# Attention with top-k and a highway layer: two heads stacked on the partitions of kT and qT, score matmuls alternating between the two 64-row halves of the array

## Chip, cores and metric

One core of a Trainium2 chip runs the whole program. The metric is device microseconds of one execution. The kernel before takes 1702.07 us (median of 2 runs, 1701.22 to 1702.92). All single times below are in us.

## The reference, cut to what matters

```python
B, H, S, D = 8, 8, 576, 64                      # q, k, v in fp32
scores = scale * q @ k^T                        # per batch and head: 576 x 576
kth    = 32nd largest of each row
mask   = scores >= kth
attn   = softmax(where(mask, scores, -1e9))     # only 32 entries per row survive
x      = attn @ v        -> rows of B*S, 512 columns (all heads side by side)
out    = T * relu(x @ w_h) + (1 - T) * x,   T = sigmoid(x @ w_t + b_t)
```

The 32nd largest value decides exactly which scores survive, so scores stay in fp32.

## The kernel before

A query tile is 128 rows of one head (the last tile of a batch holds 64 rows of two heads). There are 288 such tiles, worked on in groups of three. Where 40 query tiles are counted below, one is the same rows for all eight heads (five in each of eight batches). For each tile VectorE (DVE) finds the 32nd largest value with four `max` (8 values each) and three `match_replace`, then multiplies the exponentials by the mask:

```python
def prep_head(prep, stages, h):                    # k and q of one head -> kT, qT
    for src_t, dst_t in ((kin, kT), (qin, qT)):
        for g0 in range(0, nck, 4):                # 512 columns, then 64
            kqps = fps.tile([P, max(dm, 512)], FP32, tag="fp")    # ONE buffer
            for c in range(g0, g1):
                nc.tensor.transpose(kqps[0:D, ...], src_t[0:kc, c, :], ident_f[...])
            nc.scalar.copy(dst_t[0:D, h, col0:col1], kqps[0:D, 0 : col1 - col0])

def attn_scores(b, qt, heads, kT, qT, tix):
    ps = bigps.tile([P, nck * P], FP32, tag="big")                # two buffers
    # ... for every head, s0 in (0, 512):
        nc.tensor.matmul(ps[...], qT[0:D, h, qs : qs + qlen], kT[0:D, h, s0:s1])
    nc.scalar.copy(sc, ps)                                        # scores to SBUF
    nc.scalar.activation(e, ps, AF.Exp, scale=scale)

# chain_emitter, on DVE: max, match_replace, max, match_replace, max, match_replace, max
nc.vector.scalar_tensor_tensor(out=ep, in0=sc, scalar=m4[:, 7:8], in1=e,
                               op0=ALU.is_ge, op1=ALU.mult)       # "the mask", line 218
nc.gpsimd.memset(ep[0:nrows, S : nck * P], 0.0)

# ... transposes of ep, product with v, and for a finished 128-row tile of all heads:
nc.vector.reciprocal(...); nc.vector.tensor_scalar_mul(rinv, rinv, 0.5)
nc.gpsimd.tensor_tensor(x, xs, rinv.to_broadcast(...), ALU.mult)
# FFN: 4 transposes (xtps), 4 matmuls (hps), 5 matmuls (tps), all in the "fp" buffer; then
nc.gpsimd.tensor_add(s1, h2, x)                   # four GpSimd ops with two SBUF inputs
nc.gpsimd.tensor_sub(h2, h2, x)
nc.gpsimd.tensor_mul(h2, h2, tt)
nc.gpsimd.tensor_add(o, s1, h2)
nc.gpsimd.dma_start(out_rows, o)
```

The loads of k, q and v of the next batch stand at the end of the first query tile of a batch (the later ones wait until staging memory comes free), and `prep_head` of the next batch is spread over its second and third query tiles, between the other work. The program fixes the order of TensorE's instructions.

The softmax here doesn't subtract the row's maximum and nothing guards it: scores larger than these inputs give would overflow.

## Time and profile before

| | before |
|---|---|
| time | 1702.07 |
| span in the profile | 1701.3 |
| DVE busy | 1633.3 (96%) |
| TensorE busy | 1304.4 (77%) |
| start-up idle of DVE (first five waits for scores) | 44.4 |
| the 288 masks on DVE | 241.8 |

The busy line of the page of the kernel before:

```profile
PE 1304.4 (77%) x5448; PEld 671.2 (39%) x5480; DVE 1633.3 (96%) x3248; ACT 730.9 (43%) x1529; POOL 436.1 (26%) x732
```

The view of waits of DVE in the kernel before (what waited, on whom: us in total, times, longest):

```profile
DVE m_396 L197 <- ACT sc L188: 29.7, 1, 29.7
DVE m_398 L197 <- ACT sc L188: 5.0, 1, 5.0
DVE m_400 L197 <- ACT sc L188: 5.0, 1, 5.0
DVE m_565 L197 <- ACT sc L188: 3.9, 1, 3.9
DVE rinv_all L266 <- ACT xs L259: 3.9, 1, 3.9
DVE m_981 L197 <- ACT sc L188: 0.8, 1, 0.8
```

These are all waits of DVE in the whole run. Five lie at the start (44.4 us together) and one at the end. From 113 us, where the wait of 0.8 us ends, to the last group DVE never waits. So a change pays only if it shortens the start, the tail, or the DVE instructions themselves.

The groups of the page that the change touches (line, engine, op, names, shapes, count; then busy us, mean ns; then idle before them and who ended it):

```profile
L181 PE MATMUL ps<-kT,qT 64*128 64x512 f32 (+3 forms) x1280 | 720.1, 723 | 8.3 <-ACT e L190 7.3
...
L160 PE MATMUL kqps<-ident_f,kin 128*64 128x128 f32 (+1 forms) x320 | 79.7, 366 | 59.3 <-ACT kT L165 29.1
L160 PE MATMUL kqps<-ident_f,qin 128*64 128x128 f32 (+1 forms) x320 | 81.8, 375 | 56.3 <-ACT qT L165 31.2
```

The score matmuls are the largest item of TensorE. The two groups of transposes are busy for 161 us, but TensorE stands idle for another 115 us just before them, mostly for the copy out of the single PSUM buffer (97 of the 115 us in the full view of these lines).

The view of one source line, the mask, over the whole run (window, DVE busy and count, then clock, DMA share, GB/s):

```profile
0.00:1702.00 1702.00, 241.79 (x288) 0.59 0.11 22
```

And the timeline around one finished query tile of the kernel before (start, length, engine, line, op; "idle before" in brackets; lines between left out):

```profile
619.06 0.18 DVE L266 RECIPROCAL rinv_all<-xs 128x8 f32<-128x8 f32 x1
...
627.95 1.26 POOL L318 TENSOR_TENSOR s_5360<-h_5356,x 128x512 f32<-128x512 f32 x1
629.29 1.27 POOL L319 TENSOR_TENSOR h_5356<-h_5356,x 128x512 f32<-128x512 f32 x1
...
633.10 1.26 POOL L320 TENSOR_TENSOR h_5356<-h_5356,tt 128x512 f32<-128x512 f32 x1 [2.54 <-ACT xs L259]
...
633.67 1.30 DVE L218 SCALAR_TENSOR_TENSOR ep<-sc,m_5430,e 128x576 bf16<-128x576 f32 x1
...
634.44 1.66 POOL L322 TENSOR_TENSOR o<-s_5360,h_5356 128x512 f32<-128x512 f32 x1
...
634.90 1.82 DVE L218 SCALAR_TENSOR_TENSOR ep<-sc,m_5432,e 128x576 bf16<-128x576 f32 x1
...
636.64 0.80 DVE L218 SCALAR_TENSOR_TENSOR ep<-sc,m_5434,e 128x576 bf16<-128x576 f32 x1
```

The third mask, with no FFN op beside it, takes 0.80 us. The first two overlap the last two FFN ops on GpSimd (POOL) and take 1.30 and 1.82 us. DVE counts this as busy time, so no wait shows it. The rule is in the Trainium skill, "SBUF — State Buffer", section "Who interferes with whom": a DVE instruction with two SBUF inputs contends with a GpSimd instruction that reads SBUF. This trace agrees: the mask has two such inputs (sc and e).

Two things decide when the FFN's ops run on GpSimd. The first is when x starts. In the program, the pad writes of the mask tiles (line 227) stand before x on GpSimd, and by the page they wait for TensorE's transposes of finished masks (line 238). In one tile whose reciprocal starts at 278.76 us, TensorE first prepares k and q of the next batch (until 282.84), and x starts 5.4 us after the reciprocal instead of 1.0 (page, then timelines):

```profile
L227 POOL MEMSET ep<- 128x64 bf16 x288 | 43.2, 155 | 1106.5 <-PE etall L238 1067.4
...
282.77 1.25 PE L238 MATMUL etall<-ident_b,ep 128*128 128x128 bf16 x10
...
284.08 0.15 POOL L227 MEMSET ep<- 128x64 bf16 x1 [0.38 <-PE etall L238]
284.19 1.03 POOL L269 TENSOR_TENSOR x<-xs,rinv_all 64x512 f32<-64x512 f32 x1
```

The second is how long TensorE takes for the FFN's products once x is there.

### The profile page before, as it was taken

To read this page: it belongs to the slowest core of one execution; us is meant where nothing else is said; L and a number is where in the kernel's file an instruction comes from. 1 tells how busy PE (TensorE), PEld (TensorE's weight loads), DVE (VectorE), ACT (ScalarE), POOL (GpSimd) and SP (SyncE) were. 2 spreads that over 40 slices of the span, in tenths; PEclk is the share of its full clock that TensorE was granted. 3 is DMA by queue.
4 is the path that set the end of the run, shared out by engine and by line. 5 is a ranking of instruction groups with operands and counts; after the bars stand their busy time and mean duration, and the time that the engine had idled before them with its cause. 6 is when DMAs were issued, how large, how long until landed. Compare 5 with 4: busy or idle time off the path is not lost.

```text
span 1701.3 us, 18714 instructions
## 1 busy us (share of the span) xinstructions
PE 1304.4 (77%) x5448; PEld 671.2 (39%) x5480; DVE 1633.3 (96%) x3248; ACT 730.9 (43%) x1529; POOL 436.1 (26%) x732
## 2 busy tenths in 40 slices
PE   3888877888678876889768886788877888686653
PEld 1444433443334433444334443344433443343322
DVE  0899999999999999999999999999999999999994
ACT  2445444553335543455335543455443544343432
POOL 7001125012340133321141111511115112131133
PEclk9997656555555565555555555555555555555555
DMA  7110002100110002110021000210002000000000
GB/s 132 39 32 28 7 8 27 31 28 7 15 27 23 28 11 16 34 31 14 7 18 42 28 7 7 28 31 28 7 7 28 25 7 7 7 10 1 7 13 10
DMA packets 71829, 36.60 MB, mean 22 GB/s; under 512 B 51888, under 2 KB 68272, under 8 KB 71728
## 3 DMA queue, kind: packets, MB, share of 16 engines
q0 software_dynamic: 41856, 14.17, 6.0%
q1 hardware_dynamic: 15008, 10.76, 2.2%
q10 hardware_dynamic: 14864, 10.49, 2.2%
q8 instruction: 44, 0.72, 0.2%
q14 instruction: 57, 0.47, 0.1%
HBM read 30.67 MB, written 9.44 MB: 24 GB/s over the span
## 4 chain that ended last, share of the span: by engine, by line
DVE 55%; PE 24%; issue 9%; POOL 5%; ACT 4%; ACTq 1%; DMA 1%; DVEq 0%; POOLq 0%
PE ps L181 11%; DVE ep L218 7%; PE kqps L160 5%; PE etall L238 2%; PE etall L251 2%; PE hps L290 1%; ACT qT L165 1%; POOL vbraw L128 1%; ACT kT L165 1%; PE tps L299 1%; POOL vbraw L139 1%; POOL vbraw L118 1%; PE xtps L280 1%; ACTq L128 1%; DMA wh_76<-in_moe_w_h_dram 0%
## 5 line engine op out<-in xcount | busy, mean ns | idle before, releaser
L181 PE MATMUL ps<-kT,qT 64*128 64x512 f32 (+3 forms) x1280 | 720.1, 723 | 8.3 <-ACT e L190 7.3
L238 PE MATMUL etall<-ident_b,ep 128*128 128x128 bf16 x1440 | 195.9, 304 | 221.2 <-DVE ep L218 218.5
L181 PEld LDWEIGHTS ps<-kT,qT 64*128 64x128 f32 (+1 forms) x1280 | 285.7, 283 | 198.3 <-issue 158.2
L227 POOL MEMSET ep<- 128x64 bf16 x288 | 43.2, 155 | 1106.5 <-PE etall L238 1067.4
L188 ACT COPY sc<-ps 128x576 f32<-128x576 f32 x288 | 186.3, 647 | 304.7 <-DVE ep L218 258.3
L238 PEld LDWEIGHTS <-ep 128*128 128x128 bf16 x1440 | 138.9, 137 | 275.0 <-DVE ep L218 239.3
L245 ACT COPY et<-etall 128x640 bf16<-128x640 bf16 x288 | 192.5, 697 | 74.5 <-PE etall L238 72.3
L190 ACT ACTIVATE e<-ps 128x576 bf16<-128x576 f32 x288 | 191.9, 666 | 0.0
L251 PEld LDWEIGHTS <-et 128*128 128x128 bf16 (+1 forms) x1600 | 101.2, 134 | 124.8 <-issue 36.4
L251 PE MATMUL etall<-vbraw,et 128*128 128x65 bf16 (+1 forms) x1600 | 124.3, 242 | 10.3 <-ACT et L245 9.9
L160 PE MATMUL kqps<-ident_f,kin 128*64 128x128 f32 (+1 forms) x320 | 79.7, 366 | 59.3 <-ACT kT L165 29.1
L160 PE MATMUL kqps<-ident_f,qin 128*64 128x128 f32 (+1 forms) x320 | 81.8, 375 | 56.3 <-ACT qT L165 31.2
L165 ACT COPY kT<-kqps 64x512 f32<-64x512 f32 (+1 forms) x128 | 50.3, 393 | 119.3 <-PE kqps L160 116.2
L259 ACT COPY xs<-etall 128x65 f32<-128x65 f32 (+1 forms) x288 | 59.8, 221 | 80.5 <-PE etall L251 77.1
L165 ACT COPY qT<-kqps 64x512 f32<-64x512 f32 (+1 forms) x128 | 50.2, 393 | 95.3 <-PE kqps L160 90.7
L160 PEld LDWEIGHTS kqps<-ident_f,kin 128*64 128x64 f32 (+1 forms) x320 | 39.7, 143 | 110.8 <-ACT kT L165 45.9
L160 PEld LDWEIGHTS kqps<-ident_f,qin 128*64 128x64 f32 (+1 forms) x320 | 41.4, 148 | 95.3 <-ACT qT L165 53.0
L316 ACT ACTIVATE tt<-tps 128x512 f32<-128x512 f32 (+1 forms) x40 | 23.8, 596 | 123.7 <-PE tps L306 123.7
L290 PE MATMUL hps<-wh,xT 128*128 128x512 bf16 (+1 forms) x128 | 67.2, 614 | 7.7 <-issue 6.8
L299 PE MATMUL tps<-wt,xT 128*128 128x512 bf16 (+1 forms) x160 | 65.2, 553 | 2.0 <-ACT h_14371 L314 0.7
L280 PEld LDWEIGHTS xtps<-ident_f,x 128*128 128x128 f32 (+1 forms) x160 | 27.7, 216 | 75.6 <-POOL x L269 70.0
L280 PE MATMUL xtps<-ident_f,x 128*128 128x128 f32 (+1 forms) x160 | 40.5, 407 | 20.2 <-POOL x L269 19.2
(3393 smaller groups left out, 2328.6 us busy)
## 6 DMA issues: line engine op xcount, KB each, us to landing
kin<-in_k_dram SPq DMA_DIRECT2D x64, 128.0 KB, 2.0
qin<-in_q_dram ACTq DMA_DIRECT2D x64, 128.0 KB, 2.1
out_dram<-o POOLq DMA_DIRECT2D x32, 256.0 KB, 2.6
vbraw<-in_v_dram POOLq DMA_DIRECT2D x64, 64.0 KB, 2.7
wt_79<-in_moe_w_t_dram ACTq DMA_DIRECT2D x1, 1024.0 KB, 9.4
wh_76<-in_moe_w_h_dram SPq DMA_DIRECT2D x1, 1024.0 KB, 8.3
kin<-in_k_dram ACTq DMA_DIRECT2D x64, 16.0 KB, 2.2
qin<-in_q_dram SPq DMA_DIRECT2D x64, 16.0 KB, 2.3
```

Source lines behind the costliest of these rows:

```text
L160: nc.tensor.transpose(kqps[0:D, (c - g0) * P : (c - g0) * P + kc], src_t[0:kc, c, :], ident_f[0:kc, 0:kc],)
L165: nc.scalar.copy(dst_t[0:D, h, col0:col1], kqps[0:D, 0 : col1 - col0])
L181: nc.tensor.matmul(ps[r0 : r0 + qlen, s0:s1], qT[0:D, h, qs : qs + qlen], kT[0:D, h, s0:s1],)
L188: nc.scalar.copy(sc[0:nrows, :], ps[0:nrows, 0:S])
L190: nc.scalar.activation(e[0:nrows, :], ps[0:nrows, 0:S], AF.Exp, scale=scale)
L218: nc.vector.scalar_tensor_tensor(out=ep[0:nrows, 0:S], in0=sc[0:nrows, :], scalar=m4[0:nrows, 7:8], in1=st["e"][0:nrows, :], op0=ALU.is_ge ...
L238: nc.tensor.transpose(etall[0:P, c * P : c * P + nrows], ep[0:nrows, c * P : (c + 1) * P], ident_b[0:nrows, 0:nrows],)
L245: nc.scalar.copy(et[0:P, 0:nck, 0:nrows], etps_v[0:P, 0:nck, 0:nrows])
L251: nc.tensor.matmul(pso[0:qlen, gi * DE : (gi + 1) * DE], et[0:P, c, q0 : q0 + qlen], vb[0:P, h, c, :], start=(c == 0), stop=(c == nck - 1),)
L280: nc.tensor.transpose(xtps[0:P, g * P : g * P + qlen], x[0:qlen, g * P : (g + 1) * P], ident_f[0:qlen, 0:qlen],)
L290: nc.tensor.matmul(hps[0:qlen, 0:dm], xT[0:P, g, 0:qlen], wh[0:P, g, 0:dm], start=(g == 0), stop=(g == n_g - 1),)
L299: nc.tensor.matmul(tps[0:qlen, 0:dm], xT[0:P, g, 0:qlen], wt[0:P, g, 0:dm], start=(g == 0), stop=False,)
```

## The change

The intent: a contraction of 64 rows fills half of the array. With an even head on rows 0 to 63 and its odd neighbour on rows 64 to 127, the score matmuls of the two heads can go to different halves and overlap. Staging two heads side by side also lets one transpose of 128 columns prepare both heads.

```diff
-        for h in range(H):
-            kin = ldpool.tile([P, nck, D], FP32)
-            qin = ldpool.tile([P, nck, D], FP32)
+        for hp in range(NHP):
+            kin = ldpool.tile([P, nck, 2, D], FP32)
+            qin = ldpool.tile([P, nck, 2, D], FP32)
+            for hh in range(2):
+                h = 2 * hp + hh
+                load_head(k, kin[:, :, hh, :], b, h, (nc.sync, nc.scalar))
+                # ... q and v alike
     def prep_alloc(b):
-        kT = kqpool.tile([D, H, S], FP32)
+        kT = kqpool.tile([P, NHP, S], FP32)
     # prep_head becomes prep_pair
                     nc.tensor.transpose(
-                        kqps[0:D, ...], src_t[0:kc, c, :], ident_f[0:kc, 0:kc])
-                nc.scalar.copy(dst_t[0:D, h, col0:col1], kqps[0:D, 0 : col1 - col0])
+                        kqps[:, ...], src_t[0:kc, c, :, :].rearrange("p h d -> p (h d)"), ...)
+                nc.scalar.copy(dst_t[:, hp, col0:col1], kqps[:, 0 : col1 - col0])
+    def score_pieces(qt, qlen, hp, outs, kT, qT):
+        for s0 in range(0, S, 512):
+            for hh in range(2):
+                r = slice(hh * D, (hh + 1) * D)
+                nc.tensor.matmul(outs[hh][:, s0:s1], qT[r, hp, qs : qs + qlen], kT[r, hp, s0:s1])
     # attn_scores: an even head takes both PSUM buffers and issues the pair's pieces,
     # the odd head finds its scores ready (cut)
     # schedule of the next batch's preparation: pairs instead of heads (cut)
```

The DVE instructions are the same in number and order.

More of the change, by code (lines that the diff above doesn't have):

```diff
@@ L133, in load_batch @@
         vb = vbraw[:, :, 0 : nck * DE].rearrange("p h (c e) -> p h c e", e=DE)
-        for h in range(H):
-            kin = ldpool.tile([P, nck, D], FP32)
-            qin = ldpool.tile([P, nck, D], FP32)
-            load_head(k, kin, b, h, (nc.sync, nc.scalar))
-            load_head(q, qin, b, h, (nc.scalar, nc.sync))
-            nc.gpsimd.memset(vbraw[:, h, :], 1.0)
-            load_head(v, vb[:, h, :, 0:D], b, h, (nc.gpsimd, nc.gpsimd))
+        for hp in range(NHP):
[4 more added lines that the diff above has]
+                load_head(k, kin[:, :, hh, :], b, h, (nc.sync, nc.scalar))
+                load_head(q, qin[:, :, hh, :], b, h, (nc.scalar, nc.sync))
+                nc.gpsimd.memset(vbraw[:, h, :], 1.0)
+                load_head(v, vb[:, h, :, 0:D], b, h, (nc.gpsimd, nc.gpsimd))
             stages.append((kin, qin))
@@ L144, in prep_alloc, with prep_pair @@
     def prep_alloc(b):
-        kT = kqpool.tile([D, H, S], FP32)
-        qT = kqpool.tile([D, H, S], FP32)
+        kT = kqpool.tile([P, NHP, S], FP32)
+        qT = kqpool.tile([P, NHP, S], FP32)
         return kT, qT
-    def prep_head(prep, stages, h):
+    def prep_pair(prep, stages, hp):
         kT, qT = prep
-        kin, qin = stages[h]
+        kin, qin = stages[hp]
         for src_t, dst_t in ((kin, kT), (qin, qT)):
@@ L160, in prep_head, with evac @@
                     nc.tensor.transpose(
-                        kqps[0:D, (c - g0) * P : (c - g0) * P + kc],
-                        src_t[0:kc, c, :],
+                        kqps[:, (c - g0) * P : (c - g0) * P + kc],
+                        src_t[0:kc, c, :, :].rearrange("p h d -> p (h d)"),
                         ident_f[0:kc, 0:kc],
                     )
-                nc.scalar.copy(dst_t[0:D, h, col0:col1], kqps[0:D, 0 : col1 - col0])
+                nc.scalar.copy(dst_t[:, hp, col0:col1], kqps[:, 0 : col1 - col0])
     def prep_batch(b, stages):
         prep = prep_alloc(b)
-        for h in range(H):
-            prep_head(prep, stages, h)
-        return prep
-    def attn_scores(b, qt, heads, kT, qT, tix):
-        qs = qt * P
-        qlen = chunk_len(qt)
-        ps = bigps.tile([P, nck * P], FP32, tag="big")
-        for gi, h in enumerate(heads):
-            r0 = gi * P2 if len(heads) > 1 else 0
-            for s0 in range(0, S, 512):
-                s1 = min(S, s0 + 512)
-                nc.tensor.matmul(
-                    ps[r0 : r0 + qlen, s0:s1],
-                    qT[0:D, h, qs : qs + qlen],
-                    kT[0:D, h, s0:s1],
-                )
-        nrows = P if len(heads) > 1 else qlen
+        for hp in range(NHP):
+            prep_pair(prep, stages, hp)
+        return prep
+    def evac(ps, nrows, tix):
         sc = scpool.tile([P, S], FP32, tag=f"sc{tix % NROT}")
@@ L190, in attn_scores @@
         nc.scalar.activation(e[0:nrows, :], ps[0:nrows, 0:S], AF.Exp, scale=scale)
-        return dict(sc=sc, e=e, nrows=nrows, qlen=qlen, heads=heads)
+        return sc, e
+    def score_pieces(qt, qlen, hp, outs, kT, qT):
+        qs = qt * P
+        for s0 in range(0, S, 512):
+            s1 = min(S, s0 + 512)
+            for hh in range(2):
+                r = slice(hh * D, (hh + 1) * D)
+                nc.tensor.matmul(
+                    outs[hh][:, s0:s1],
+                    qT[r, hp, qs : qs + qlen],
+                    kT[r, hp, s0:s1],
+                )
+    def attn_scores(b, qt, heads, kT, qT, tix):
+        qlen = chunk_len(qt)
+        hp = heads[0] // 2
+        if len(heads) > 1:
+            ps = bigps.tile([P, nck * P], FP32, tag="big")
+            score_pieces(qt, qlen, hp, [ps[0:P2, :], ps[P2:P, :]], kT, qT)
+            sc, e = evac(ps, P, tix)
+            return dict(sc=sc, e=e, nrows=P, qlen=qlen, heads=heads)
+        if heads[0] % 2 == 0:
+            pss = []
+            for hh in range(2):
+                ps = bigps.tile([P, nck * P], FP32, tag="big")
+                pss.append(ps)
+            score_pieces(qt, qlen, hp, [pss[0][0:qlen, :], pss[1][0:qlen, :]], kT, qT)
+            pend_ps[(b, qt, heads[0] + 1)] = pss[1]
+            ps = pss[0]
+        else:
+            ps = pend_ps.pop((b, qt, heads[0]))
+        sc, e = evac(ps, qlen, tix)
+        return dict(sc=sc, e=e, nrows=qlen, qlen=qlen, heads=heads)
+    pend_ps = {}
     def chain_emitter(st, tix):
@@ L350, in ensure_prep @@
                 stages, vb = stg.pop(b)
-                for hh in range(hdone, H):
-                    prep_head(prep, stages, hh)
+                for hh in range(hdone, NHP):
+                    prep_pair(prep, stages, hh)
                 preps[b] = (prep[0], prep[1], vb)
@@ L387, in prefetch_hooks @@
                 partial[b + 1] = [prep_alloc(b + 1), 0]
-            want = min(H, (0 if qt == 1 else NHP) + (lasth + 1 + 1) // 2)
+            want = min(NHP, (0 if qt == 1 else NHP // 2) + (lasth + 1) // 4)
             prep, hdone = partial[b + 1]
@@ L391, in prefetch_hooks @@
             while hdone < want:
-                prep_head(prep, stages, hdone)
+                prep_pair(prep, stages, hdone)
                 hdone += 1
             partial[b + 1] = [prep, hdone]
-            if hdone == H:
+            if hdone == NHP:
                 vb_next = stg.pop(b + 1)[1]
```

## The prediction

> **What bounds the kernel now.** VectorE. The busy table has DVE at 1633.3 us of 1701.3 (96%); in the windows 400-1000 and 1000-1600 us it is busy 600.00 of 600. Its 68 us of idle time lie at the two ends: the view of waits shows 44.4 us before the top-k chain settles (29.7 us to the first max, then 5.0, 5.0, 3.9, 0.8), the rest is the tail of about 22 us after the last mask (last FFN, output). TensorE is busy 77% of the span, nearly all of it under DVE, so the score matmuls (line 181, 1280 of them, 720 us) are off the critical path in steady state.
>
> **What the change does.**
> - Transposes into kT/qT: 640 become 320, their PSUM copies 256 become 128 (393 ns each, 50.3+50.2 us): about 80 us of PE and 50 us of ACT removed. Off the path except at the start.
> - Score matmuls: same 1280, now from rows 0-63 and 64-127. The Trainium skill (TensorEngine Tiling (Array Packing), Theoretical Speedup) gives up to 2x for contraction of 64 or less; I expect less: the built order mostly puts one head's 512 and 64 columns back to back and the other head after a wait for its PSUM buffer. Worth nothing on the path.
> - DVE: same instructions, same order.
> - Loads: kin/qin now hold two heads interleaved, so a k or q load of 128 rows x 1 KB becomes 512 pieces of 256 B: per batch 3072 descriptors become 9216. In the trace the 1 KB pieces cost about 40 ns of an engine each (q1: 368 packets, 1.0% of 16 engines over 95 us). If 256 B pieces cost 20 to 30 ns (estimate from v's small pieces, 31 ns in the stretch 20-30 us), k and q of one batch go from about 8 to about 14 us of all 16 engines, on top of v's 19 us. At the start the engines are already 90% busy (20 to 30 us); later 10%.
> - Four buffers now hold four pairs: in the built order ACT issues 16 loads, each waiting for earlier ones, before its first PSUM copy (before: 8, copy at 21.8 us). I expect that copy at 33-40 us, the first max at 40-48 us instead of 29.7.
> - In return scores come two heads at a time: the later start-up gaps (14.7 us) shrink to about 5.
>
> **Sum.** Start-up idle 44 us becomes about 52 (45 to 63): +8. DVE work is unchanged but for collisions with GpSimd: the mask (line 218) takes 0.8 us, but up to 1.82 us where FFN tensor ops on GpSimd overlap it, some 21 us in total over the run. The Trainium skill (SBUF — State Buffer, Who interferes with whom) says a DVE op with two SBUF inputs contends with GpSimd reading SBUF; the trace agrees. FFN may finish earlier: -2. Tail unchanged.
>
> Predicted 1709 us, range 1697 to 1725. Faster by over 2%: 0.01; within 2%: 0.95; slower by over 2%: 0.04.
>
> **What would show it.** DVE busy still about 1630 and 100% busy from 400 to 1600; first max later than 36 us, remaining start gaps under 8 us together; ACT copies of kT/qT 128; under-512 B packets up by some 65,000; PE share down to about 70%; mask total near 240 us.
>
> **What would make it wrong.** Slow loads stalling ACT in steady state (DVE gaps once per batch); a pair holding both PSUM buffers starving DVE; fast 256 B loads, so the start gets earlier; collisions vanishing or doubling (up to 20 us either way).

## More of the kernel before

In the tile at 619.06 us x is on time, and two blocks of score matmuls stand between the products (xtps, hps and tps; lines between left out):

```profile
622.78 2.50 PE L181 MATMUL ps<-kT,qT 64*128 64x64 f32 x4
...
627.57 2.50 PE L181 MATMUL ps<-kT,qT 64*128 64x64 f32 x4
630.01 1.89 PE L299 MATMUL tps<-wt,xT 128*128 128x512 bf16 x4
```

## The result, and the profile after

1688.38 us (median of 2 runs, 1688.06 to 1688.70), against 1702.07. The ratio is 0.9924, 95% interval 0.9895 to 0.9953; it is not quite the ratio of these medians, which is 0.9920. (In the experiments below, a ratio is the mean of one kernel's fast runs over the mean of the other's fast runs of the same rounds.) The change gains 0.8%, inside 2% but outside the predicted range.

| | before | after |
|---|---|---|
| span in the profile | 1701.3 | 1686.9 |
| DVE busy | 1633.3 | 1619.1 |
| TensorE busy | 1304.4 | 1204.1 |
| start-up idle of DVE | 44.4 | 44.2 |
| the 288 masks | 241.8 | 230.7 |
| the 40 multiplies of rinv on DVE | 9.8 | 6.0 |

The busy line of the page of the changed kernel:

```profile
PE 1204.1 (71%) x5128; PEld 587.0 (35%) x5160; DVE 1619.1 (96%) x3248; ACT 678.8 (40%) x1401; POOL 424.5 (25%) x732
```

The view of waits of DVE in the changed kernel:

```profile
DVE m_316 L221 <- ACT sc L177: 39.8, 1, 39.8
DVE m_320 L221 <- ACT sc L177: 4.0, 1, 4.0
DVE rinv_all L290 <- ACT xs L283: 3.9, 1, 3.9
DVE m_318 L221 <- ACT sc L177: 0.4, 1, 0.4
```

The first scores arrive 10 us later, but the gaps that follow are 10 us shorter. The start costs the same: 39.8 + 4.0 + 0.4 = 44.2 us.

The groups of the changed kernel that answer to those of before:

```profile
L188 PE MATMUL ps<-kT,qT 64*128 64x64 f32 (+3 forms) x1280 | 692.0, 724 | 33.2 <-ACT e L179 32.8
...
L162 PE MATMUL kqps<-ident_f,kin 128*128 128x128 f32 (+1 forms) x160 | 38.7, 351 | 46.6 <-ACT kT L167 22.4
L162 PE MATMUL kqps<-ident_f,qin 128*128 128x128 f32 (+1 forms) x160 | 42.1, 380 | 37.8 <-ACT qT L167 23.1
```

The score matmuls, the target of the change, went from 720.1 to 692.0 us of TensorE's busy time: 4%, nothing like a half. Each has two records in the trace. Of the 1,024 records of the tiles with 128 rows, 129 start within 20 ns of the score record before them (none in the kernel before), so the two halves do run together, but seldom. The busy time of the transposes halved, and the idle time before them fell from 115.6 to 84.4 us.

The view of the mask line over the whole run of the changed kernel:

```profile
0.00:1687.00 1687.00, 230.70 (x288) 0.58 0.12 22
```

And the timeline of the same query tile (the thirteenth) in the changed kernel:

```profile
618.13 0.19 DVE L290 RECIPROCAL rinv_all<-xs 128x8 f32<-128x8 f32 x1
...
626.60 1.27 POOL L342 TENSOR_TENSOR s_5040<-h_5036,x 128x512 f32<-128x512 f32 x1 [0.27 <-ACT h_5036 L338]
627.95 1.27 POOL L343 TENSOR_TENSOR h_5036<-h_5036,x 128x512 f32<-128x512 f32 x1
629.29 1.27 POOL L344 TENSOR_TENSOR h_5036<-h_5036,tt 128x512 f32<-128x512 f32 x1
630.64 1.26 POOL L346 TENSOR_TENSOR o<-s_5040,h_5036 128x512 f32<-128x512 f32 x1
...
632.75 0.80 DVE L242 SCALAR_TENSOR_TENSOR ep<-sc,m_5110,e 128x576 bf16<-128x576 f32 x1
633.46 0.81 DVE L242 SCALAR_TENSOR_TENSOR ep<-sc,m_5112,e 128x576 bf16<-128x576 f32 x1
...
634.19 0.81 DVE L242 SCALAR_TENSOR_TENSOR ep<-sc,m_5114,e 128x576 bf16<-128x576 f32 x1
```

The last FFN op now ends 13.8 us after the reciprocal instead of 17.0, and the next masks start 14.6 us after it in both kernels. The whole FFN fits before the masks, and all three take 0.8 us. In both kernels x starts 1.0 us after the reciprocal here, so the gain of this tile lies between x and the tanh, in the score matmuls between the FFN's products and in the last product:

```profile
621.86 2.08 PE L188 MATMUL ps<-kT,qT 64*128 64x64 f32 x4
...
626.05 1.12 PE L188 MATMUL ps<-kT,qT 64*128 64x512 f32 x2
627.10 1.04 PE L323 MATMUL tps<-wt,xT 128*128 128x512 bf16 x4
```

This is no exception. In the first three query tiles of the first seven batches the mean from the end of x to the start of the tanh fell from 10.8 to 9.1 us. In that time TensorE runs no transpose of the preparation in either kernel; its score matmuls take 4.9 us before and 3.6 after, and the last product (tps) 1.9 and 1.5 us; why tps is shorter was not examined. Over all 40 query tiles the mean end of the FFN on GpSimd went from 17.9 to 14.7 us after the reciprocal, and the tiles whose FFN ends after the next masks begin (later than 14.65 us; the last two tiles of the run aside) went from 34 to 16.

Where do the overlaps vanish? The table sorts the masks' time above 0.8 us, in us, by the query tile whose FFN ran beside them (masks over 0.83 us; one profiled execution of each kernel):

| query tiles, sorted by x in the kernel before | before | after | e3 | e4 (a fast run) | e12 | e14 |
|---|---|---|---|---|---|---|
| 20 with x on time | 19.0 | 4.6 | 6.0 | 2.9 | 6.5 | 4.8 |
| 14 with x over 2 us late | 3.6 | 1.3 | 2.6 | 4.5 | 9.4 | 7.0 |
| the fourth of six batches, x late in all kernels | 2.9 | 8.4 | 4.2 | 8.1 | 6.1 | 8.7 |
| together | 25.5 | 14.4 | 12.8 | 15.6 | 22.1 | 20.5 |

So the gain lies in tiles whose x was on time already. The other columns are used with the experiments.

Masks give 11.1 us. The small multiply of rinv has one SBUF input, but it too was longer in ten tiles of before (9.79 against 5.96 us for 40): five times beside an FFN op (0.61 to 1.16 instead of 0.15 us) and five times beside the instructions on GpSimd that issue the loads of v and set their buffer (0.34 to 0.36 us). Why it is held up is not shown here. Together 14.9 us, which is the fall of DVE's busy time (14.2 us; instructions overlap a little at their ends).

### The profile page after: what moved, and what is told of

Read it like the earlier page. It is cut to its first block, busy times and chain, and to the rows that moved or that the text cites. A ratio compares the mean times of both kernels' runs of the same rounds, so it can differ in the third digit from the quotient of the medians.

```text
span 1686.9 us, 17781 instructions
## 1 busy us (share of the span) xinstructions
PE 1204.1 (71%) x5128; PEld 587.0 (35%) x5160; DVE 1619.1 (96%) x3248; ACT 678.8 (40%) x1401; POOL 424.5 (25%) x732
## 2 busy tenths in 40 slices
DMA packets 120977, 36.55 MB, mean 22 GB/s; under 512 B 117424, under 2 KB 117424, under 8 KB 120880
## 4 chain that ended last, share of the span: by engine, by line
DVE 77%; issue 9%; PE 8%; DMA 2%; ACT 1%; POOL 1%; ACTq 1%; DVEq 0%; SPq 0%; POOLq 0%
DVE ep L242 9%; PE ps L188 4%; PE kqps L162 1%; DMA kin<-in_k_dram 1%; PE etall L275 1%; PE hps L314 1%; PE tps L323 1%; PE etall L262 1%; DMA wh_76<-in_moe_w_h_dram 0%; ACTq L128 0%; ACT kT L167 0%; ACT qT L167 0%; ACT e L179 0%; PE xtps L304 0%; DVE rinv_all L290 0%
## 5 line engine op out<-in xcount | busy, mean ns | idle before, releaser
L188 PE MATMUL ps<-kT,qT 64*128 64x64 f32 (+3 forms) x1280 | 692.0, 724 | 33.2 <-ACT e L179 32.8
L188 PEld LDWEIGHTS ps<-kT,qT 64*128 64x128 f32 (+1 forms) x1280 | 242.6, 277 | 190.3 <-issue 117.3
L262 PEld LDWEIGHTS <-ep 128*128 128x128 bf16 x1440 | 133.7, 135 | 413.8 <-DVE ep L242 348.8
L162 PE MATMUL kqps<-ident_f,kin 128*128 128x128 f32 (+1 forms) x160 | 38.7, 351 | 46.6 <-ACT kT L167 22.4
L162 PE MATMUL kqps<-ident_f,qin 128*128 128x128 f32 (+1 forms) x160 | 42.1, 380 | 37.8 <-ACT qT L167 23.1
L323 PE MATMUL tps<-wt,xT 128*128 128x512 bf16 (+1 forms) x160 | 57.6, 497 | 2.0 <-ACT h_13731 L338 0.7
L293 POOL TENSOR_TENSOR x<-xs,rinv_all 128x512 f32<-128x512 f32 (+1 forms) x40 | 41.7, 1042 | 46.6 <-DVE rinv_all L291 35.4
L118 POOL DMA_DIRECT2D vbraw<-in_v_dram x64 | 50.0, 782 | 1.9 <-issue 1.9
L167 ACT COPY kT<-kqps 128x512 f32<-128x512 f32 x64 | 25.6, 399 | 58.8 <-PE kqps L162 53.8
L162 PEld LDWEIGHTS kqps<-ident_f,kin 128*128 128x128 f32 (+1 forms) x160 | 23.0, 173 | 73.8 <-ACT kT L167 30.7
```

The costliest lines, as they stand in the source:

```text
L162: nc.tensor.transpose(kqps[:, (c - g0) * P : (c - g0) * P + kc], src_t[0:kc, c, :, :].rearrange("p h d -> p (h d)"), ident_f[0:kc, 0:kc],)
L188: nc.tensor.matmul(outs[hh][:, s0:s1], qT[r, hp, qs : qs + qlen], kT[r, hp, s0:s1],)
L262: nc.tensor.transpose(etall[0:P, c * P : c * P + nrows], ep[0:nrows, c * P : (c + 1) * P], ident_b[0:nrows, 0:nrows],)
L323: nc.tensor.matmul(tps[0:qlen, 0:dm], xT[0:P, g, 0:qlen], wt[0:P, g, 0:dm], start=(g == 0), stop=False,)
```

## The experiments

The 15 runs use three theories at first. **C**: the gain is fewer overlaps of DVE with GpSimd's FFN, and nothing else. **P**: those overlaps fell because preparing pairs holds TensorE up less. **T**: they fell because the score matmuls alternate on the halves of the array. All times are medians; the kernel before was timed in the same rounds, and its medians were 1701.27 (e1 to e4), 1700.62 (e5 to e8), 1702.34 (e9 to e11) and 1705.41 (e12 to e15). Each of these four groups ran on another chip.

### e1 and e2: both kernels without the four GpSimd ops of the FFN (wrong results on purpose)

```diff
-        nc.gpsimd.tensor_add(s1, h2, x)   # and tensor_sub, tensor_mul, tensor_add
-        nc.gpsimd.dma_start(out_rows_ap(b, qt, qlen), o[0:qlen, :])
+        nc.gpsimd.dma_start(out_rows_ap(b, qt, qlen), tt[0:qlen, :])
```

> The kernel before without the four GpSimd tensor ops of the FFN (tanh result is stored, a wrong result on purpose). Theory C (the change pays by fewer overlaps of DVE's mask and of the small DVE multiply with GpSimd's FFN ops): mask total falls from 241.8 to about 220 us, DVE busy from 1633 to about 1604, time about 1672 us (1667 to 1678). Rival S (the change pays because scores reach DVE sooner or DVE does less): time stays within 4 us of 1702 less a few us of tail.

> The changed kernel without the same four GpSimd ops (wrong on purpose). Theory C: the advantage of the change vanishes, time within 3 us of e1_nopool_before, about 1672 us; mask total about 220 us as there. Rival S: it stays about 14 us faster than e1_nopool_before.

Measured: 1669.42 (e1, 1668.69 to 1670.29) and 1669.20 (e2, 1669.11 to 1669.88). Their outputs are wrong, which doesn't matter for the times. The groups of DVE in e1 and in e2:

```profile
L218 DVE SCALAR_TENSOR_TENSOR ep<-sc,m,e 128x576 bf16<-128x576 f32 x288 | 216.1, 800 | 0.0
```

```profile
L242 DVE SCALAR_TENSOR_TENSOR ep<-sc,m,e 128x576 bf16<-128x576 f32 x288 | 216.0, 800 | 0.0
```

Every mask takes 800 ns in both, and the whole advantage of the change is gone: 0.2 us are left of 13.7. Theory C holds, and the start-up and the tail are shown to be neutral. What the overlaps cost is read from DVE's busy time: 28.4 us in the kernel before (1633.3 less 1604.9 in e1) and 14.4 us in the changed kernel (1619.1 less 1604.7 in e2). The times fall by more (1701.27 to 1669.42 is 32 us), because the last FFN of the run also has four ops fewer: from the last mask to the end it is 24.1 us in the kernel before and 18.8 in e1 (24.1 and 19.3 for the changed kernel and e2).

### e3: pair preparation without interleaved scores

The changed kernel's loads, transposes and copies, with the scores of one head at a time in the old order:

```diff
-            score_pieces(qt, qlen, hp, [pss[0][0:qlen, :], pss[1][0:qlen, :]], kT, qT)
+        for gi, h in enumerate(heads):
+            r = slice((h % 2) * D, (h % 2 + 1) * D)
+            # for s0: nc.tensor.matmul(ps[...], qT[r, h // 2, ...], kT[r, h // 2, s0:s1])
```

> Pair loads, pair transposes and copies as in the changed kernel, but scores one head at a time in the old order. Theory P (fewer transposes and copies take the TensorE backlog away, so FFN and its GpSimd ops come earlier): 1687 to 1692 us, mask total near 231 us, x on GpSimd about 1 us after the reciprocal in most tiles. Rival T (paired score matmuls on the two array halves are what helps): within 3 us of 1702.

Measured: 1686.47 (1685.12 to 1687.18), ratio to before 0.991; masks 229.1 us. This is the whole gain and a little more (start-up idle is 41.8 us, 2.4 less than in the changed kernel), without interleaving the score matmuls of two heads. I read it as theory P at first, but it does not exclude T: odd heads still lie on rows 64 to 127, 84 of the 1,024 score records start within 20 ns of the one before, and from x to the tanh it is 9.5 us with 3.9 us of score matmuls, as in the changed kernel rather than as before. So e3 shows that interleaving isn't needed. Pair preparation with all heads on one half was not run.

### e4: alternating scores alone

The kernel before with kT and qT stacked by the copy (an odd head is copied from PSUM rows 0 to 63 to SBUF rows 64 to 127), and paired scores. A first build that transposed odd heads straight to PSUM rows 64 to 127 did not compile ("PSUM partition on transpose matrix multiplication outputs must be 0, got partition 64 instead"). This fits the Trainium skill: "TensorEngine Tiling (Array Packing)", section "Restrictions and Gotchas", lists fp32 transposes among what column tiling excludes.

```diff
-                nc.scalar.copy(dst_t[0:D, h, col0:col1], kqps[0:D, ...])
+                nc.scalar.copy(dst_t[r, h // 2, col0:col1], kqps[0:D, ...])    # r: rows of h % 2
```

> Loads and transposes per head as before (copies put odd heads on rows 64 to 127), scores paired as in the changed kernel. Theory P: 1697 to 1704 us, TensorE still late at the first tiles of a batch. Rival T: 1685 to 1691 us, mask total near 231 us.

Measured: median 1693.03, but the six runs are 1686.38, 1688.47, 1688.89, 1697.16, 1702.62 and 1702.72; ratio 0.9957 (0.9924 to 0.999). Neither theory expected such a spread. In three executions alternating scores give the whole gain or nearly (the profiled run, at 1688.89, has masks of 232.1 us, and x starts more than 2 us after the reciprocal in 7 of 40 tiles), in two they give nothing, and one lies between. The kernel before spreads too (1698.56 to 1708.81 in these rounds). In the profiled run the preparation is as before, and yet from x to the tanh it is 9.0 us with 3.6 us of score matmuls, and the 20 tiles with x on time have lost their overlaps (19.0 to 2.9 us). So the two halves can give the gain without pair preparation (theory T), but only in part of the runs.

### e5 and e6: two PSUM buffers for transposes and FFN, in both kernels

```diff
-    fps = ctx.enter_context(tc.tile_pool(name="fps", bufs=1, space=bass.MemoryType.PSUM))
+    fps = ctx.enter_context(tc.tile_pool(name="fps", bufs=2, space=bass.MemoryType.PSUM))
```

> The kernel before with two PSUM buffers instead of one for transposes and FFN products; no transposes removed, scores as before. In its instruction order the two FFN products now stand back to back on TensorE with no score matmul between. Theory C with P (time is set by when GpSimd's FFN ops fall against the mask): FFN ends about 3 us earlier after the reciprocal, TensorE no longer waits for a copy between transposes; mask total falls from 241.8 to below 228 us, time 1676 to 1690 us. If only the removed transposes count: within 4 us of 1701.

> The changed kernel with two such PSUM buffers. Theory C: no FFN op on GpSimd reaches the next mask (last op ends under 14.6 us after the reciprocal in nearly all tiles), mask total about 218 us, time 1670 to 1676 us. Then the change is worth only what is left between e5 and e6.

Measured: 1681.76 (e5) and 1681.88 (e6), each within 0.6 us of its median. One line turns the kernel before into one that beats the change; in e5 it is 7.9 us from x to the tanh, with 2.5 us of score matmuls. For e6 my expectation missed by 6 us. In e6 the masks are 223.8 us (e5: 230.5), so the overlaps still fell by 6.7 us, though not to 218; but start-up idle is 43.5 us in e6 and 36.8 in e5, which gives the same 6.7 us back. The second buffer speeds up the kernel before at the start, where the change gains little from it (44.2 to 43.5 us). The overlaps that remain in e6 all come from the FFN of the fourth query tile of a batch: there GpSimd is still issuing the loads of v for the next batch, one after the other, when x could begin (in the first batch until 264.1 us, with the reciprocal at 260.9).

### e7, e8 and e14: which part of the preparation counts

All three start from e3 and double the transposes (e7), the copies (e8), or both (e14).

```diff
+                    for _rep in range(2):              # e7, e14
                         nc.tensor.transpose(kqps[:, ...], ...)
                 nc.scalar.copy(dst_t[:, hp, col0:col1], kqps[...])
+                nc.scalar.copy(dst_t[:, hp, col0:col1], kqps[...])     # e8, e14
```

> e3_pairprep_only with every pair transpose issued twice (640 again, as in the kernel before; copies stay at 128). If the removed TensorE work is the cause: back to 1695 to 1702 us. If the halved copies and round trips between TensorE and ScalarE are the cause: 1685 to 1690 us.

> e3_pairprep_only with every PSUM copy of kT and qT issued twice (256 again; transposes stay at 320). If round trips and ScalarE time are the cause: back to 1694 to 1702 us. If TensorE work is the cause: 1685 to 1690 us.

> e3_pairprep_only with every pair transpose and every copy doubled: as many transposes and copies as before (640 and 256) in 16 round trips per batch. Theory R (round trips): 1688 to 1696 us, of which up to 8 us at the start, mask total at most 233 us. Theory W (the summed work of TensorE and ScalarE in the preparation): 1698 to 1706 us, mask total near 242 us.

Measured: e7 1689.66 (masks 228.2, start-up idle 45.6), e8 1688.43 (229.5, 44.5), e14 1698.46 (236.6, 46.7). e3 had 229.1 and 41.8. So neither the transposes nor the copies alone bring the overlaps back; what e7 and e8 lose to e3 is their longer start. Both together bring back more than half of what e3 gains in the masks. e14 missed both of my ranges for the mask, between R and W, and its time is at the lower edge of W.

### e9, e12 and e13: more round trips

From e3: one PSUM tile and one copy per 128 columns.

```diff
-            for g0 in range(0, nck, 4):
-                g1 = min(nck, g0 + 4)
+            for g0 in range(0, nck, 1):
+                g1 = min(nck, g0 + 1)
```

> e3_pairprep_only with one PSUM tile and one copy for every 128 columns, so 40 round trips between TensorE and ScalarE per batch (before: 32, e3: 16, e7 and e8: 16); transposes stay at 320. Theory R (before's delay comes from the number of round trips during the preparation of the next batch, in which TensorE waits in order): mask total back near 242 us, DVE busy about 1632 us, time 1697 to 1706 us. If round trips don't matter: 1684 to 1691 us, mask total near 229 us.

> e9_roundtrips once more for a profile, because e9 has runs near 1694 and runs near 1703 us and its profile is of one near 1694. If this execution is near 1703: theory C says DVE busy about 1631 us and a mask total near 240 us, start idle as in e9 (47.5). If the 9 us lie elsewhere (start or tail): mask total stays near 232.

> The same kernel again, a second draw of the same question: near 1703 us the mask total should be near 240 us and DVE busy near 1631 us; near 1694 us it should be 232 and 1622.

Measured: e9 median 1702.75, in two clusters: 1694.16 and 1694.69, and 1702.74 to 1704.66. Its profile is of the run at 1694.69. e12 and e13 are single profiled runs of the same kernel, at 1700.38 and 1694.42; the state of a single run is unknown, but both times lie within the fast runs of e9. The DVE group of the mask in e13 is 232.2 us as in e9; in e12 it is:

```profile
L223 DVE SCALAR_TENSOR_TENSOR ep<-sc,m,e 128x576 bf16<-128x576 f32 x288 | 238.3, 878 | 0.0
```

DVE busy is 1628.3 in e12 and 1621.9 in e13, start-up idle 47.0 and 47.2. So two executions of the same program differ by 6.0 us, and the mask by 6.1 us: in this pair the overlaps are also what makes the runs scatter. e12 reached 1700.4 and not the upper cluster at 1703, which fits a mask below the 240 that I had expected for 1703. Even at its best e9 loses 5.7 us of start and 3.1 us of masks to e3.

Why do e9 and e14 lose masks and e7 and e8 not? TensorE in the kernel before, during the preparation of the next batch (timeline, TensorE only):

```profile
299.68 1.06 PE L160 MATMUL kqps<-ident_f,kin 128*64 128x128 f32 x4 [0.69 <-ACT qT L165]
301.41 0.31 PE L160 MATMUL kqps<-ident_f,kin 64*64 64x64 f32 x1 [0.67 <-ACT kT L165]
302.53 1.06 PE L160 MATMUL kqps<-ident_f,qin 128*64 128x128 f32 x4 [0.81 <-ACT kT L165]
304.26 0.31 PE L160 MATMUL kqps<-ident_f,qin 64*64 64x64 f32 x1 [0.67 <-ACT qT L165]
304.50 0.40 PE L238 MATMUL etall<-ident_b,ep 128*128 128x128 bf16 x2
305.26 1.06 PE L160 MATMUL kqps<-ident_f,kin 128*64 128x128 f32 x4 [0.36 <-ACT qT L165]
306.11 1.06 PE L238 MATMUL etall<-ident_b,ep 128*128 128x128 bf16 x8
```

One head takes about 5 us (299.68 to 304.57), of which transposes are about half; the rest is waiting for the copy that frees the one buffer. In TensorE's order of instructions the transposes of finished masks (line 238) stand behind it. In the timelines I joined the instructions on kqps between 255 and 380 us to stretches (gaps under 5 us closed) and added their lengths:

| run | stretches of preparation, us | masks, us |
|---|---|---|
| after | 17.5 | 230.7 |
| e3 pair preparation | 18.8 | 229.1 |
| e7 transposes doubled | 22.5 | 228.2 |
| e5 before with two buffers | 24.1 | 230.5 |
| e8 copies doubled | 28.8 | 229.5 |
| e9, e12 more round trips | 38.5, 38.4 | 232.2, 238.3 |
| e14 both doubled | 39.1 | 236.6 |
| e4 alternating scores alone (a fast run) | 42.3 | 232.1 |
| before | 44.3 | 241.8 |

The runs with at most 28.8 us of preparation have masks of 228.2 to 230.7 us, those with 38 us and more 232.1 to 241.8. So the length of the hold-up sorts these runs better than the number of one kind of instruction, and e3, e7, e8, e9, e12 and e14 have the same score matmuls: within them a longer preparation brings overlaps back (in e12 and e14 mostly in the 14 tiles whose x was late in before). But the length does not decide alone: e9 and e12 have the same length and differ by 6.1 us in the mask, and e4, with its heads on two halves, has nearly the length of before and 9.7 us less. What decides there, and into which cluster a run of e4 or e9 falls, remains open. e5 also gives the FFN products a second buffer, so its masks are not owed to the preparation alone.

### e10: the same change with four heads staged ahead

```diff
-    ldpool = ctx.enter_context(tc.tile_pool(name="ld", bufs=4))
+    ldpool = ctx.enter_context(tc.tile_pool(name="ld", bufs=2))
```

> The changed kernel with two staging buffers of two heads (four heads ahead, as in the kernel before) instead of four. If the 16 loads that ScalarE issues before its first copy set the start: first max at about 32 to 34 us instead of 39.8, start idle 38 to 42 us instead of 44.2, time 1683 to 1687 us. If the arrival of the first pair's data sets it: first max stays at 38 to 40 us.

Measured: 1678.77 (1677.15 to 1679.40), ratio 0.9853: 4 us better than I expected at best. First max at 29.9 us, start-up idle 34.7 us (44.2 after), masks 229.5. ScalarE's first copy comes at 22.4 us, after 8 loads, instead of 30.1 us after 16. The change had doubled the bytes per staging buffer and left the count at 4; that alone cost about 9.5 us.

### e11 and e15: a version that takes the other costs away too

From the changed kernel: loads of the first batch issued before the weights, which get staging memory of their own (before, the k and q tiles reused the weights' staging memory, so no k or q load started before 14.4 us); k and q loads on the SP queue only; two "fp" PSUM buffers as in e6; the zero pad of the eight mask tiles written once. e15 is the same with e3's scores.

```diff
+    stg[0] = load_batch(0)
+    eps = [...]                                   # 8 tiles, pad set to zero once
+    wtmp = ctx.enter_context(tc.tile_pool(name="wtmp", bufs=1))    # weights after
-                load_head(k, kin[:, :, hh, :], b, h, (nc.sync, nc.scalar))
+                load_head(k, kin[:, :, hh, :], b, h, (nc.sync, nc.sync))
-        nc.gpsimd.memset(ep[0:nrows, S : nck * P], 0.0)
+        ep = eps[tix % NROT]
```

> The changed kernel with the two remaining costs taken away: first loads start at about 1 us (weights staged in memory of their own and loaded after), k and q loads on the SP queue only, two PSUM buffers for transposes and FFN, the zero pad of the eight mask tiles set once so that GpSimd doesn't wait there. Expected: first max at 16 to 22 us instead of 39.8, mask total 216 to 220 us, time 1648 to 1660 us. Against: if early loads don't help or other overlaps come up, 1665 us or more.

> e11_best with the scores of one head at a time instead of alternating halves. If the alternating score matmuls bring nothing to the time: within 3 us of e11_best, 1653 to 1659 us. If they help: 1660 us or more.

Measured: e11 1655.77 (1655.59 to 1656.67), ratio 0.9721, faster; e15 1655.69 (1655.62 to 1655.80). Both results are correct. The waits of DVE in e11 (scores at the start, and the one at the end):

```profile
DVE m L205 <- ACT sc L161: 21.4, 2, 20.7
DVE rinv_all L272 <- ACT xs L265: 3.6, 1, 3.6
```

The masks are 218.7 us in both. The start gives 22.8 us (44.2 to 21.4) and the fewer overlaps about 10 (DVE busy 1619.1 to 1608.7): together 33.2 us, against the 32.6 us between the medians of the changed kernel and e11. Again interleaving the two heads' score matmuls brings nothing to the time. In e11 the pad write is gone from the loop; x still starts 3.2 to 4.2 us after the reciprocal in the fourth query tile of six batches, behind the loads of v. Which of e11's changes took the masks from 223.8 us (e6) to 218.7 was not tried one by one.

## Why the prediction was wrong

- **What bounds the kernel: right.** DVE stays at 100% between the ends in both traces, and TensorE's own time is under it.
- **Transposes, copies, packets: right.** 128 copies instead of 256, TensorE at 71%, and 65,536 more packets under 512 B (51,888 to 117,424; "some 65,000").
- **Score matmuls "worth nothing on the path": right for interleaving, doubtful for the halves.** e3 and e15 have the time without interleaved pieces. The reason given holds: the pieces of two heads are mostly not side by side in the built order (129 of 1,024 records start together), and busy time fell by 4% only. The skill's "Theoretical Speedup" of up to 2x in "TensorEngine Tiling (Array Packing)" is for tiles that run together; no run here measures that factor. But score matmuls stand between the FFN's products, so they decide when GpSimd's ops run: 4.9 us of them from x to the tanh before, 3.6 after, and e4 has the gain in some executions with the old preparation.
- **"Start-up idle 44 us becomes about 52 (45 to 63): +8": too large by 8 us.** The mechanism was right: the first copy waits for 16 loads, the first max is late (39.8 us; "40-48"), the later gaps shrink (4.4 us; "about 5"). The size was off: the first copy came at 30.1 us instead of 33 to 40. A likely reason, which no run isolates, is that pieces of 256 B cost less than the "20 to 30 ns" that I put in. In the trace's DMA records of q1 in the changed kernel the packets under 300 B take 17.8 ns in mean; in the kernel before the 1 KB packets take 54 ns. So 1 KB in four pieces costs about 1.3 times as much (4 x 17.8 = 71 ns). The Trainium skill would have told me nearly that: "DMA: Bandwidth & Descriptors", section "Why small descriptors are slow (HBM only)", gives 256/32 + 3 = 11 cycles for 256 B. My estimate from that page: 4 x 11 = 44 cycles against 1024/32 + 3 = 35 for 1 KB, a factor of 1.26.
- **"FFN may finish earlier: -2": the step that failed.** It gave about -14.9 in the trace: 11.1 us of masks and 3.8 us of the rinv multiply. The mechanism was named, and the overlaps were measured ("some 21 us in total"; e1 shows 25.7 in the masks), but the prediction gives no working for the 2 us. It treated TensorE's work as off the path, the score matmuls and the preparation ("off the path except at the start"). Both are off the chain of data that bounds DVE, but they decide when GpSimd runs, and GpSimd's timing lengthens DVE's instructions. e1 and e2 show that the overlaps are the whole gain. How they fell is read from the traces. First and most: from x to the tanh TensorE takes 9.1 instead of 10.8 us, as score matmuls take less of it; in the 20 tiles with x on time the masks' excess fell from 19.0 to 4.6 us. Second: x starts on time in 14 of the 20 tiles where it was over 2 us late, because TensorE is held up less by the preparation; there the excess fell from 3.6 to 1.3 us. (In the other six tiles GpSimd is still issuing the loads of v in both kernels, and the excess rose from 2.9 to 8.4 us.) No run separates the halves from pair preparation in all executions: e3 has both, and e4, with the halves alone, has the gain in part of its runs.
- **"Collisions vanishing or doubling (up to 20 us either way)"** stood among what would make the prediction wrong, and the range of 1697 to 1725 left no room for it. A term of 21 us known to depend on phase needed a range of that size downwards.

## What to carry to other kernels

When one engine is 100% busy, look for instructions of it that take different times at the same shape: here 0.8 and 1.82 us, which no wait shows. Find what other engine runs beside the slow ones, and ask for the whole chain what moves that engine in time; work that is off the critical chain can then decide the time through an overlap. Take the overlap away by construction (as in e1 for a measurement, or a second buffer and no needless wait as in e6 and e11) before tuning by chance, and when a staging tile doubles in size, reconsider the number of its buffers and how many loads stand ahead of the first use in an engine's queue.

## What the Trainium skill lacked or had wrong

- "SBUF — State Buffer", "Who interferes with whom", states the contention, and these traces agree: masks of 0.80 us alone and up to 1.82 us beside a GpSimd op with two SBUF inputs. It has no size for a whole kernel; here it was about 28 us of 1701 (DVE busy 1633.3 us, 1604.9 without the four ops).
- No page says that this contention makes execution times of one program scatter: two executions of the kernel of e9 differed by 6.0 us and their masks by 6.1 us, and in the same rounds the kernel before spread from 1698.71 to 1709.38 (11 runs) while e11, with few overlaps left, spread by 1.1 us (5 runs).
- "TensorEngine Tiling (Array Packing)" gives a theoretical factor of up to 2 for contraction of 64. It doesn't say in which instruction order that factor is had; here, with 129 of 1,024 records starting within 20 ns of the one before, busy time of the score matmuls went from 720.1 to 692.0 us.
